# The opening of a one-core dynamic convolution with gated projection: softmax by lane, late zeros, x and weights in a new order, a buffer for the first group's rows

## The chip, the cores and the metric

One core of a Trainium2 chip runs the whole program. The time is the device time of one execution in microseconds (us), from fixed fp32 and 64-bit inputs in HBM to the fp32 result in HBM; three runs of the kernel before are given.

## The reference, cut to what matters

With B = 8 lanes of S = 4224 rows, D = 192 channels, H = 8 heads of 24 channels, K = 7 taps drawn per row and head, and 5 fixed taps per channel:

```
w   = softmax(weight_gen[b, s, h, :])                       # over 7 taps (the sum has 1e-9 added)
a   = sum_k w[b,s,h,k] * x[b, s-6+k, 24 channels of h]      # rows before 0 are zero
g   = sigmoid(sum_j conv_w[j] * a[b, s-4+j, :])             # 5 taps, per channel
out = (g * (a @ w_val)) @ w_out                             # 192 x 192 matrices
```

`conv_w`, `w_val` and `w_out` arrive as 64-bit floats and are turned into fp32 on the chip with integer operations.

## The kernel before, in words

**Work units.** The 4224 rows are cut into 36 groups: 80 rows, then 34 groups of 120, then 64. Two neighbouring groups make a pair (`Pair`); the first and the last group stand alone, so there are 19 pairs, 0 to 18. All 8 lanes go through a group together.

**Softmax parts.** Eleven `Softmax` parts `s0` to `s10` turn `weight_gen` into normalised taps. A part is loaded (`wt`), worked in place (max, subtract, exp on ScalarE, sum, reciprocal, multiply), gets its neighbours' edge rows (`halo`, L238, an SBUF to SBUF transfer), is spread into a padded layout (`spread`, L251, four copies), and stored to a DRAM buffer `z` (`store`, L265, four transfers). `s0` is worked in two halves of its rows (`h0`, `h1`), each with both of the two lanes that a partition holds. `s0` and `s1` are spread into parts of the tile `aA`, all later ones into `zt`. Rows of `z` end in a gap that must be zero; `clear_z` writes these from a zero tile.

**Banded weights and the first product.** `load_t` (L300, 7 or 9 transfers for a group) reads `z` with overlapping rows into one of two tiles `tb`, which gives a banded matrix; the parts of `tb` outside the band are cleared once (`tb_clear`). `load_x` brings the rows of `x` into one of three tiles `xt`. `bank` (L339) multiplies them, 128 small matmuls in four banks for a group, and `evac` (L354, ScalarE) copies the banks to `S`, `ringB`, `ringA`, `ringA`. The channels do not fit 128 partitions evenly: part of them goes by way of `S`, from which `move` (L362, L364, twelve transfers for a pair, GpSimd's queue) puts them into holes of the two rings. There is one `S`, and its next copy waits until the moves have read it.

**The second half of a pair, one and two steps later.** `tap0` (ScalarE, L380) and four `tap` (VectorE, L384) make the gate sum in `aA` and `aB`, `sigm` (L389) the sigmoid; `wva_`, `wvb_`, `wvm_`, `wvd_` (TensorE) the product with `w_val`; `gv` (VectorE, L435 to L443) multiplies the two and frees the banks `ps0` and `ps1`, which the next pair's `bank` writes; `omA` and `omB` (L451, L460) the product with `w_out`; `oev` and `store` take it out.

**Weights.** `order_weights` (six transfers, DRAM to DRAM), `load_weights` (six transfers, which wait for the first six), `convert_weights` (three blocks of eight VectorE operations), `place_weights` (ten ScalarE copies).

**Order.** Nothing is scheduled by a planner: every call `at(t, ...)` adds a step, the steps are sorted by their number t and issued in that order, and each engine works its own in order. SyncE, ScalarE and GpSimd each have a queue that issues transfers, and a transfer that waits holds up all that follows on its engine. Pairs have `when(q)` = 25, 30, 54, 79, then 24.5 more for each. The opening (L532 to L601) is written out by hand. In the opening before, GpSimd has the weights' twelve transfers ahead of `x`; SyncE has the loads of `s0`, `s1`, `s2` and both zeroings of `z` ahead of the first store.

Of the kernel before, what the change touches and what calls it, by code (L numbers as in the profile page):

```python
# [16 lines left out]
def tile_dynconv_gated_moe(  # L17
# [16 lines left out]
    P = 128  # L34
# [147 lines left out]
    class Softmax:  # L182
# [15 lines left out]
        def load(self, eng, lo=0, hi=None):  # L198
            R, n = self.R, (hi or self.m) - lo
            src = bass.AP(tensor=wg.tensor, offset=wg.offset + (self.r0 + lo) * ROW,  # L200
                          ap=[[R * ROW, NBL], [LQ * S * ROW, NL], [S * ROW, LQ], [1, n * ROW]])
            w = self.wt[:, 0:1]
            dst = bass.AP(tensor=w.tensor, offset=w.offset + lo * ROW,
                          ap=[[w.ap[0][0], P], [self.n * ROW, LQ], [1, n * ROW]])
            eng.dma_start(out=dst, in_=src)

        def own(self, lo=0, hi=None):
            hi = hi or self.m
            w = self.wt[:, :, lo:hi].rearrange("p l r (h k) -> p l (r h) k", k=K)
            m = self.mx[:, :, H * lo:H * hi]  # L210
            return w, m, m.unsqueeze(3).broadcast_to([P, LQ, (hi - lo) * H, K])

        def max(self, *rows):
            w, m, _ = self.own(*rows)
# [100 lines left out]
    class Pair:  # L315

        def __init__(self, q, ms):
            self.q, self.g = q, [gr[m] for m in ms]
            self.s = self.g[0].s
            self.n = sum(g.n for g in self.g)  # L320
            self.base = SLOT * (q % 2) + HALO
            self.lp = LH // len(self.g)
            self.w = self.lp * self.n
            self.pieces = LH // self.lp
            self.aA = aAs[(q + 2) % 3][:, 0:L * self.n]
            self.aB = aBs[q % 3][:, 0:LH * self.n]
# [17 lines left out]
        def evac(self, gi, kind, b):  # L344
# [188 lines left out]
    half = s0.m // 2  # L533
    h0, h1 = (0, half), (half, s0.m)
# [6 lines left out]
    at(0.3, clear_z, 0, 0, 320, SP)  # L541
    at(0.35, s2.load, SP)
# [74 lines left out]
    for q, pr in enumerate(pairs + [None, None]):  # L617
# [33 lines left out]
        if p1:  # L651
# [6 lines left out]
            st(6.5, p1.wvm_)  # L658
# [47 lines left out]
```

## Time and profile before

| | us |
|---|---|
| median of 3 runs (527.23, 529.28, 530.59) | 529.28 |
| the profiled execution, its own time | 531.67 |
| span of the profiled execution | 529.9 |
| VectorE busy | 425.9 (80%) |
| TensorE busy / weight loads | 457.3 (86%) / 334.9 (63%) |
| ScalarE busy / GpSimd busy | 314.8 (59%) / 312.9 (59%) |

All times in the text are us from the start of the span of this one execution. Over the whole span a mean share hides that the program has an opening, in which the first groups are prepared, and then a repeated pattern of pairs; the two are read apart by asking for windows of the span. An engine name with a q (SPq, ACTq, POOLq) is that engine's queue issuing a transfer; DVE is VectorE, ACT ScalarE, POOL GpSimd, SP SyncE, PE TensorE.

### The profile page before, as it was taken

The numbers are of one execution on the slowest core, as the hardware profiler recorded it, in microseconds if no ns is written. First come the engines' busy times: TensorE is split into PE (matmuls) and PEld (weight loads), VectorE is DVE, ScalarE is ACT, GpSimd is POOL, SyncE is SP. The second block draws the span as 40 slices with busy tenths as digits, with TensorE's granted clock in tenths as the row PEclk, the third lists the DMA queues.
The fourth block names the chain that finished last, engine by engine and source line by source line (L and its number), as shares of the span: only waits on it lengthen the run. The fifth ranks groups of instructions, "written<-read, shape, count | busy, mean of one in ns | idle before, by whom it ended". The sixth has DMA issues, their size and how long they took to land.

```text
span 529.9 us, 15947 instructions
## 1 busy us (share of the span) xinstructions
PE 457.3 (86%) x6546; PEld 334.9 (63%) x6546; DVE 425.9 (80%) x351; ACT 314.8 (59%) x434; POOL 312.9 (59%) x546
## 2 busy tenths in 40 slices
PE   7016569597979999999799999999899999999996
PEld 3016455556667767685668575868485858586584
DVE  5856749998978798889789897999699959695960
ACT  5513584766466747664766667675758474655532
POOL 8768597447563847384747566574738384816400
PEclk9557779799979999999999999999999999999999
DMA  8987878778888778968888888789786968664344
GB/s 252 220 220 195 195 222 210 210 159 228 274 238 198 206 250 232 224 188 268 226 231 223 244 239 220 230 242 251 214 263 173 264 177 245 163 185 103 93 113 114
DMA packets 90935, 111.33 MB, mean 210 GB/s; under 512 B 18473, under 2 KB 79248, under 8 KB 90862
## 3 DMA queue, kind: packets, MB, share of 16 engines
q1 hardware_dynamic: 67516, 73.14, 49.3%
q0 software_dynamic: 21904, 35.95, 26.6%
q10 hardware_dynamic: 1442, 1.21, 1.1%
q8 instruction: 52, 0.85, 0.7%
q14 instruction: 21, 0.17, 0.1%
HBM read 59.80 MB, written 41.17 MB: 191 GB/s over the span
## 4 chain that ended last, share of the span: by engine, by line
PE 31%; issue 21%; POOL 18%; DMA 13%; DVE 9%; ACT 7%; POOLq 0%; ACTq 0%; DVEq 0%
PE ps L339 11%; PE ps L451 8%; POOL xt L286 8%; PE ps L460 5%; DMA ringA<-S 5%; POOL ringA L362 5%; POOL ringB L364 4%; DMA xt<-in_x_dram 4%; DVE aA L435 3%; PE ps L416 3%; DVE aB L443 3%; ACT aA L389 2%; DVE aA L384 2%; PE ps L411 1%; DMA wt<-wt 1%
## 5 line engine op out<-in xcount | busy, mean ns | idle before, releaser
L339 PE MATMUL ps<-tb,xt 126*32 126x120 f32 (+2 forms) x4608 | 148.0, 287 | 52.1 <-DMA xt<-in_x_dram 26.5
L339 PEld LDWEIGHTS ps<-tb,xt 126*32 126x32 f32 x4608 | 136.3, 115 | 62.7 <-issue 41.9
L286 POOL DMA_DIRECT2D xt<-in_x_dram x272 | 158.9, 620 | 11.4 <-issue 3.2
L384 DVE SCALAR_TENSOR_TENSOR aA<-ringA,wf,aA 128x1920 f32<-128x1920 f32 (+2 forms) x76 | 157.3, 2070 | 5.7 <-DMA xt<-in_x_dram 3.6
L364 POOL DMA_DIRECT2D ringB<-S x76 | 42.1, 558 | 149.0 <-ACT ringB L354 99.3
L451 PE MATMUL ps<-wf,aA 128*120 128x192 f32 (+2 forms) x576 | 111.6, 342 | 14.1 <-DVE aA L435 7.0
L451 PEld LDWEIGHTS ps<-wf,aA 128*120 128x120 f32 (+2 forms) x576 | 93.5, 190 | 28.8 <-DVE aB L443 11.6
L466 ACT COPY ot<-ps 120x768 f32<-120x768 f32 (+2 forms) x72 | 55.9, 801 | 67.9 <-PE ps L460 57.1
L362 POOL DMA_DIRECT2D ringA<-S x152 | 81.8, 544 | 17.2 <-DMA ringB<-S 6.3
L384 DVE SCALAR_TENSOR_TENSOR aB<-ringB,wf,aB 128x960 f32<-128x960 f32 (+2 forms) x76 | 86.9, 1144 | 2.0
L435 DVE TENSOR_TENSOR aA<-ps,aA 128x960 f32<-128x960 f32 (+2 forms) x36 | 39.3, 1131 | 49.9 <-ACT aA L389 29.6
L416 PE MATMUL ps<-ringA,wva 128*128 128x480 f32 (+2 forms) x144 | 61.8, 571 | 0.0
L460 PE MATMUL ps<-wf,aB 64*120 64x192 f32 (+2 forms) x576 | 60.0, 336 | 0.9 <-ACT ot L466 0.9
L460 PEld LDWEIGHTS ps<-wf,aB 64*120 64x120 f32 (+2 forms) x576 | 46.8, 183 | 17.1 <-issue 15.4
L354 ACT COPY ringA<-ps 128x480 f32<-128x480 f32 (+2 forms) x72 | 36.2, 554 | 32.7 <-PE ps L339 32.7
L380 ACT ACTIVATE aA<-ringA,wf 128x960 f32<-128x960 f32 (+2 forms) x38 | 39.1, 1031 | 18.0 <-DMA ringA<-S 18.0
L354 ACT COPY S<-ps 128x480 f32<-128x480 f32 (+2 forms) x36 | 19.9, 553 | 48.1 <-PE ps L339 41.0
L416 PEld LDWEIGHTS ps<-ringA,wva 128*128 128x128 f32 x144 | 25.8, 189 | 35.7 <-issue 21.7
L261 ACT COPY zt<-wt 128x512 f32<-128x512 f32 (+4 forms) x36 | 30.3, 920 | 15.8 <-DMA tb<-z 8.5
L411 PE MATMUL ps<-ringA,wvm 128*32 128x480 f32 (+2 forms) x304 | 33.6, 537 | 0.0
L428 PE MATMUL ps<-ringB,wvb 64*128 64x480 f32 (+2 forms) x144 | 33.5, 581 | 0.0
L389 ACT ACTIVATE aA<-aA 128x1920 f32<-128x1920 f32 (+2 forms) x19 | 32.1, 1688 | 0.8 <-DVE aA L384 0.7
(61 smaller groups left out, 358.7 us busy)
## 6 DMA issues: line engine op xcount, KB each, us to landing
xt<-in_x_dram POOLq DMA_DIRECT2D x272, 94.5 KB, 3.7
out_dram<-ot SPq DMA_DIRECT2D x68, 360.0 KB
tb<-z SPq DMA_DIRECT2D x235, 74.4 KB
z<-zt SPq DMA_DIRECT2D x28, 306.0 KB
wt<-in_weight_gen_dram SPq DMA_DIRECT2D x7, 896.0 KB
ringA<-S POOLq DMA_DIRECT2D x136, 30.0 KB, 3.6
tb<-z SPq DMA_DIRECT2D x70, 52.1 KB
wt<-wt SPq DMA_DIRECT2D x8, 294.0 KB
```

Of the source, the lines that this page charges most:

```text
L286: eng.dma_start(out=self.xb[0:G * NW, j, 0:D], in_=src)
L339: nc.tensor.matmul(out=pa[Q * c:Q * c + Q, n * l:n * l + n], lhsT=g.xb[0:k, LH * u + l, C * h:C * h + Q], rhs=t[:, (LH * u + l) // LQ, PAD ...
L354: nc.scalar.copy(out=dst, in_=pa)
L362: nc.gpsimd.dma_start(out=ringA[q:q + h, LH * u:LH * u + LH, p0:p0 + n], in_=St[p:p + h, :, 0:n])
L364: nc.gpsimd.dma_start(out=ringB[HD * u + q:HD * u + q + h, :, p0:p0 + n], in_=St[p:p + h, :, 0:n])
L384: nc.vector.scalar_tensor_tensor(out=a, in0=self.src(g, j), scalar=cw[:, g, j:j + 1], in1=a, op0=ALU.mult, op1=ALU.add)
L389: nc.scalar.activation(out=a, in_=a, func=AF.Sigmoid)
L416: nc.tensor.matmul(out=self.v01(e)[:, u], lhsT=wva, rhs=self.A(e, u), start=True, stop=False)
L435: nc.vector.tensor_tensor(out=a, in0=self.v01(e), in1=a, op=ALU.mult)
L451: nc.tensor.matmul(out=ps[b][0:n, u, D * t:D * t + D], lhsT=g[:, u, t], rhs=woa, start=first and t == 0, stop=not first, skip_group_check= ...
L460: nc.tensor.matmul(out=ps[b][0:n, u, D * t:D * t + D], lhsT=g[hs, t], rhs=wob[hs], start=first and t == 0, stop=not first, skip_group_chec ...
L466: nc.scalar.copy(out=ots[0:n, 2 * e + k], in_=ps[b][0:n, :, 0:2 * D])
```

## The change

- `s0` is worked in two halves by lane (lane 0, lane 1) and no longer by rows; each half is then one unbroken stretch of `wt` and `mx`.
- The zeros of the first `z` (rows 0 to 320) go out on ScalarE's queue after the exp of the first half; those of the second `z` (rows 0 to 256) on SyncE's queue after the loads of `tb` for group 1, its second part (rows 256 to 512) from 47.0 to `when(2) + 13`.
- `s2` is loaded after `s0`'s store; its edge rows go by SyncE and no longer GpSimd; its max to multiply come before the conversions of the weights.
- GpSimd clears all four parts of `tb0` (ScalarE cleared two), brings `x` of groups 0 and 1, clears the ring edges and `zt`, and only then orders the weights; it loads them after `s1`'s edge rows and ahead of `x` of group 2.
- Three of `s0`'s four spread copies and all four of `s1`'s are VectorE's (two and two before).
- All 24 conversions stand together at 26 to 28, ahead of `s3`'s max and subtract; `s3`'s exp stands with `s2`'s spread and `place_weights` behind group 2's `evac` and ahead of pair 0's `tap0`; `s3`'s sum stands between pair 0's taps and its `gv`, reciprocal and multiply behind that `gv`.
- Pair 0 uses the free tile `aB2` in place of `S`.

```diff
-        def load(self, eng, lo=0, hi=None):
+        def load(self, eng, l0=0, l1=LQ):
...
-        def own(self, lo=0, hi=None):
+        def own(self, l0=0, l1=LQ):
+            w = self.wt[:, l0:l1, 0:self.m].rearrange("p l r (h k) -> p l (r h) k", k=K)
+            m = self.mx[:, l0:l1]
...
+            self.S = St if q else aBs[2][:, 0:LH * self.n].rearrange("p (l n) -> p l n", n=self.n)
...
-    h0, h1 = (0, half), (half, s0.m)
+    h0, h1 = (0, 1), (1, 2)
     at(0.0, s0.load, SP, *h0)
     at(0.1, s0.load, SP, *h1)
     at(0.2, s1.load, SP)
-    at(0.3, clear_z, 0, 0, 320, SP)
-    at(0.35, s2.load, SP)
     at(0.4, lambda: G_.memset(aAt[:, 0:(s0.R + s1.R) * DATA], 0.0))
-    at(1.0, order_weights)
-    tb_clear(0, 0, 2.0, G_)
-    tb_clear(0, 1, 2.1, G_)
+    for u in range(NL):
+        tb_clear(0, u, 2.0, G_)
-    at(3.0, load_weights)
     at(4.0, gr[0].load_x, G_)
     at(5.0, gr[1].load_x, G_)
-    at(5.5, clear_z, 1, 0, 256, SP)
+    at(5.1, lambda: G_.memset(ringA[:, :, 0:HALO], 0.0))
+    at(5.1, lambda: G_.memset(ringB[:, :, 0:HALO], 0.0))
+    at(5.2, lambda: G_.memset(zt, 0.0))
+    at(5.3, order_weights)
     steps(s0, "max sub exp", 4.1, *h0)
+    at(4.13, clear_z, 0, 0, 320, A)
-    spread(s0, 11.0, (A, V, A, V))
+    spread(s0, 11.0, (A, V, V, V))
     at(11.1, s0.store, (SP, A))
-    tb_clear(0, 2, 11.5, A)
-    tb_clear(0, 3, 12.1, A)
+    at(11.2, s2.load, SP)
     at(13.0, s1.halo, (G_,))
-    at(13.1, lambda: G_.memset(ringA[:, :, 0:HALO], 0.0))
-    at(13.1, lambda: G_.memset(ringB[:, :, 0:HALO], 0.0))
+    at(13.1, load_weights)
     at(13.2, gr[2].load_x, G_)
+    tail(s3, 13.3)
...
-            at((14.0, 28.0, 29.0)[k] + 0.01 * i, lambda f=f: f(V))
-            at(t + 0.01 * w, gr[gi].load_t, s0, w, lo, hi, (SP, A)[w % 2])
-    spread(s1, 24.9, (A, A, V, V))
+            at(t + 0.01 * w, gr[gi].load_t, s0, w, lo, hi, (SP, A)[(w + (gi == 1)) % 2])
+    at(24.2, clear_z, 1, 0, 256, SP)
+    steps(s2, "max sub", 24.6)
+    at(24.8, s2.exp)
+    spread(s1, 24.9, (V, V, V, V))
+    steps(s2, "sum recip norm", 25.0)
+            at(26.0 + k + 0.01 * i, lambda f=f: f(V))
     at(28.5, s1.store, (SP,))
-    tail(s3, 26.0)
-    at(37.0, lambda: G_.memset(zt, 0.0))
+    at(29.2, s2.halo, (SP,))
     at(29.5, s3.load, SP)
-    steps(s2, "max sub", 32.5)
+    steps(s3, "max sub", 33.0)
+    spread(s2, 36.51)
-        at(33.35 + 0.001 * i, f)
-    at(32.6, s2.exp)
-    steps(s2, "sum recip norm", 32.7)
-    at(33.0, s2.halo, (G_,))
-    steps(s3, "max sub", 44.0)
-    spread(s2, 45.0)
-    at(46.0, s2.store, (SP,))
+        at(36.56 + 0.001 * i, f)
+    at(36.6, s3.exp)
+    at(36.9, s2.store, (SP,))
+    at(38.2, s3.sum)
+    steps(s3, "recip norm", 41.0)
-    at(46.9, s3.exp)
-    at(47.0, clear_z, 1, 256, 512, SP)
+    at(when(2) + 13.0, clear_z, 1, 256, 512, SP)
-    steps(s3, "sum recip norm", when(1) + 20.6)
...
-            st(6.5, p1.wvm_)
+            st(6.5 if q > 1 else 6.9, p1.wvm_)
```

## Rows read from the trace of the kernel before

**Rows 1.** Windows: length, engines' busy us, PE clock, DMA share, GB/s.
```profile
0.00:40.00 40.00, 12.21 (x130) 7.85 (x134) 25.65 (x42) 16.32 (x17) 30.89 (x51) 0.67 0.89 231
127.60:465.60 338.00, 322.20 (x4686) 236.26 (x4684) 291.70 (x209) 217.88 (x294) 202.34 (x358) 0.99 0.82 227
```
**Rows 2.** TensorE timeline: start, length, operation [idle before]; groups 0, 2, 3, 5.
```profile
37.15 4.22 PE L339 MATMUL ps<-tb,xt 126*32 126x80 f32 x128 [26.48 <-DMA xt<-in_x_dram]
...
51.43 5.22 PE L339 MATMUL ps<-tb,xt 126*32 126x120 f32 x128 [2.41 <-DMA tb<-z]
...
65.38 5.04 PE L339 MATMUL ps<-tb,xt 126*32 126x120 f32 x128 [5.74 <-DMA ringA<-S]
...
98.64 5.41 PE L339 MATMUL ps<-tb,xt 126*32 126x120 f32 x128 [5.32 <-DMA tb<-z]
```
**Rows 3.** Timeline, VectorE: the first softmax part, by halves of its rows.
```profile
6.10 1.09 DVE L215 TENSOR_REDUCE mx<-wt 128x128 f32<-128x896 f32 x1 [3.17 <-DMA wt<-in_weight_gen_dram]
...
9.32 1.09 DVE L215 TENSOR_REDUCE mx<-wt 128x128 f32<-128x896 f32 x1 [1.01 <-ACT wt L223]
...
18.32 1.09 DVE L236 TENSOR_TENSOR wt<-wt,mx 128x896 f32<-128x896 f32 x1
```
**Rows 4.** ScalarE's exp line to 60: queue waits, ns, first to last.
```profile
L223 ACTq EVENT_SEMAPHORE  x3: 17/17/17, 4.8 to 22.6; - x3
```
**Rows 5.** Timeline, SyncE's queue: first stores of z, first loads of tb.
```profile
21.03 1.22 SPq L272 DMA_DIRECT2D z<-aA  x2
28.72 9.95 SPq L313 DMA_DIRECT2D tb<-z  x9
```
**Rows 6.** Transfers in 0 to 80: count, KB each, median us to landing.
```profile
xt<-in_x_dram POOLq DMA_DIRECT2D x40, 94.5 KB, 4.7
...
z<-zero SPq DMA_DIRECT2D x2, 816.0 KB
...
ot<-cd POOLq DMA_DIRECT2D x2, 2.5 KB, 6.3
...
cd<-in_moe_conv_w_dram POOLq DMA_DIRECT2D x1, 1.9 KB, 7.1
```
**Rows 7.** Timeline, GpSimd: two clears of tb, wt's edges, pair 1's late moves.
```profile
6.74 3.72 POOL L510 MEMSET tb<- 128x2142 f32 x2
10.52 1.25 POOL L527 MEMSET wt<- 32x672 f32 x2
...
63.38 3.27 POOL L362 DMA_DIRECT2D ringA<-S  x6 [3.12 <-DMA wt<-wt]
```
**Rows 8.** VectorE timeline: conversions (first, last of 16), taps, s3, taps.
```profile
37.55 0.35 DVE L137 TENSOR_SCALAR wf<-ot 128x384 uint32<-128x384 uint32 x1
...
44.25 0.56 DVE L148 SCALAR_TENSOR_TENSOR wf<-ot,wf 128x384 uint32<-128x384 uint32 x1
...
58.71 3.65 DVE L384 SCALAR_TENSOR_TENSOR aA<-ringA,wf,aA 128x640 f32<-128x640 f32 x4 [3.64 <-DMA xt<-in_x_dram]
...
66.28 2.02 DVE L215 TENSOR_REDUCE mx<-wt 128x256 f32<-128x1792 f32 x1
...
76.93 2.02 DVE L227 TENSOR_REDUCE mx<-wt 128x256 f32<-128x1792 f32 x1 [6.58 <-ACT wt L223]
...
83.04 8.97 DVE L384 SCALAR_TENSOR_TENSOR aA<-ringA,wf,aA 128x1920 f32<-128x1920 f32 x4
```
**Rows 9.** ScalarE timeline: group 1's S, tap0, s2's spread, s3's exp.
```profile
49.25 0.56 ACT L354 COPY S<-ps 128x480 f32<-128x480 f32 x1 [7.08 <-DMA ringA<-S]
...
57.59 1.02 ACT L380 ACTIVATE aA<-ringA,wf 128x320 f32<-128x320 f32 x2
...
71.83 2.06 ACT L261 COPY zt<-wt 128x256 f32<-128x256 f32 x4
...
75.20 1.70 ACT L223 ACTIVATE wt<-wt 128x1792 f32<-128x1792 f32 x1
```
**Rows 10.** place_weights in one window: length, ScalarE busy, PE clock, DMA share, GB/s.
```profile
51.00:54.00 3.00, 1.60 (x10) 0.51 0.92 315
```

More of the change, by code (lines that the diff above doesn't have):

```diff
@@ L196, in __init__ @@
             self.z = z[:, 0:R * self.row].rearrange("p (r c) -> p r c", r=R)
-        def load(self, eng, lo=0, hi=None):
[L199 to L204, printed above, removed]
-            eng.dma_start(out=dst, in_=src)
@@ L207, in own @@
-        def own(self, lo=0, hi=None):
[L208 to L214, printed above, removed]
+        def load(self, eng, l0=0, l1=LQ):
+            R, m = self.R, self.m
+            src = bass.AP(tensor=wg.tensor, offset=wg.offset + (l0 * S + self.r0) * ROW,
+                          ap=[[R * ROW, NBL], [LQ * S * ROW, NL], [S * ROW, l1 - l0], [1, m * ROW]])
+            w = self.wt[:, l0:l0 + 1]
+            dst = bass.AP(tensor=w.tensor, offset=w.offset,
+                          ap=[[w.ap[0][0], P], [self.n * ROW, l1 - l0], [1, m * ROW]])
+            eng.dma_start(out=dst, in_=src)
@@ L215, in max, with sub @@
+        def own(self, l0=0, l1=LQ):
+            w = self.wt[:, l0:l1, 0:self.m].rearrange("p l r (h k) -> p l (r h) k", k=K)
+            m = self.mx[:, l0:l1]
+            return w, m, m.unsqueeze(3).broadcast_to([P, l1 - l0, self.m * H, K])
+        def max(self, *ls):
+            w, m, _ = self.own(*ls)
             nc.vector.tensor_reduce(out=m, in_=w, axis=AX.X, op=ALU.max)
-        def sub(self, *rows):
-            w, _, m = self.own(*rows)
+        def sub(self, *ls):
+            w, _, m = self.own(*ls)
@@ L219, in sub, with exp, sum @@
             nc.vector.tensor_tensor(out=w, in0=w, in1=m, op=ALU.subtract)
-        def exp(self, lo=0, hi=None):
-            w = self.wt[:, :, lo:hi or self.m].rearrange("p l r c -> p l (r c)")
+        def exp(self, l0=0, l1=LQ):
+            w = self.wt[:, l0:l1, 0:self.m].rearrange("p l r c -> p l (r c)")
             nc.scalar.activation(out=w, in_=w, func=AF.Exp)
-        def sum(self, *rows):
-            w, m, _ = self.own(*rows)
+        def sum(self, *ls):
+            w, m, _ = self.own(*ls)
@@ L227, in sum, with recip, norm @@
             nc.vector.tensor_reduce(out=m, in_=w, axis=AX.X, op=ALU.add)
-        def recip(self, *rows):
-            m = self.own(*rows)[1]
+        def recip(self, *ls):
+            m = self.own(*ls)[1]
             nc.vector.tensor_scalar(out=m, in0=m, scalar1=1e-9, scalar2=None, op0=ALU.add)
             nc.vector.reciprocal(out=m, in_=m)
-        def norm(self, *rows):
-            w, _, m = self.own(*rows)
+        def norm(self, *ls):
+            w, _, m = self.own(*ls)
             nc.vector.tensor_tensor(out=w, in0=w, in1=m, op=ALU.mult)
@@ L352, in evac @@
             else:
-                dst = St[:, :, p0:p0 + n]
+                dst = self.S[:, :, p0:p0 + n]
             nc.scalar.copy(out=dst, in_=pa)
@@ L361, in move @@
             if g == 0:
-                nc.gpsimd.dma_start(out=ringA[q:q + h, LH * u:LH * u + LH, p0:p0 + n], in_=St[p:p + h, :, 0:n])
+                nc.gpsimd.dma_start(out=ringA[q:q + h, LH * u:LH * u + LH, p0:p0 + n], in_=self.S[p:p + h, :, 0:n])
             else:
-                nc.gpsimd.dma_start(out=ringB[HD * u + q:HD * u + q + h, :, p0:p0 + n], in_=St[p:p + h, :, 0:n])
+                nc.gpsimd.dma_start(out=ringB[HD * u + q:HD * u + q + h, :, p0:p0 + n], in_=self.S[p:p + h, :, 0:n])
         def halo(self, g):
@@ L515, in tile_dynconv_gated_moe, with steps @@
     V, A, G_, SP = nc.vector, nc.scalar, nc.gpsimd, nc.sync
-    def steps(p, names, t, *rows):
+    def steps(p, names, t, *ls):
         for i, f in enumerate(names.split()):
-            at(t + 0.01 * i, getattr(p, f), *rows)
+            at(t + 0.01 * i, getattr(p, f), *ls)
     def spread(p, t, engs=(A, A, A, A)):
@@ L530, in tb_clear @@
         at(t, lambda: clear(tb[i], u, c0, c1, eng))
-    half = s0.m // 2
-    h0, h1 = (0, half), (half, s0.m)
+    h0, h1 = (0, 1), (1, 2)
     at(0.0, lambda: V.memset(zero, 0.0))
```

4 lines of the change are left out of this document (2 added, 2 removed).

## The prediction

> **What bounds the kernel now.** I read the windows first, the engines' timelines second, and the landings of transfers last. In the first 40 us the DMA engines are 0.89 busy at 231 GB/s while VectorE works 25.65 us of 40 and TensorE 12.21 [rows 1]: the opening waits for data. In the repeated part, 338 us for 13 pairs from pair 4's start to pair 17's, VectorE is 86% busy and TensorE 95%, at 26.0 us a pair [rows 1]. No step there reads a clock, each waits for engines and buffers; so an opening that hands over d us earlier should end d us earlier, if all that pair 3 needs comes earlier too. The change touches only the opening (and two later zeros), so I price the hand-over.
>
> The starts of the first products tell the opening's course: group 0 at 37.15, group 2 at 51.43, group 3 at 65.38, group 5 (pair 3) at 98.64 [rows 2]. Group 3 could not start before VectorE had multiplied pair 0's banks free. Group 5 followed on pair 1's gate work on VectorE, which began at 83.04 [rows 8] though pair 0's was over at 66.28 [rows 8]. What lay between is the softmax of `s3`: max and subtract from 66.28, then idle 6.58 for an exp on ScalarE, then 76.93 to 83.04 for sum, reciprocal and multiply [rows 8]. That exp, at 75.20, stood behind `s2`'s spread at 71.83 and `tap0` of pair 1 [rows 9]. From 83.04 on VectorE goes from pair to pair with taps of 9 us each [rows 8]. **The date of pair 1's taps on VectorE, 83.04, is what I forecast.**
>
> **The change part by part.**
>
> *First softmax by lane.* The first max began at 6.10, when both halves had landed, though the first had by 4.8, where ScalarE's queue passed its wait for it [rows 3, 4]; the second max waited 1.01 for the exp of the other half [rows 3], and the first sum as long again for the second exp. Halves by rows interleave in a partition; halves by lane do not, so all three waits should go: 1.3 + 1.0 + 1.0 = 3.3 us. Three spread copies on VectorE beside one on ScalarE end about when two beside two did, or 0.3 earlier: 0.2. Stores start at 17.5 and not 21.03 [rows 5]. They took 7.7 us to let the loads of `tb` go (28.72) [rows 5]; with less queued ahead it could be 5, with the zeros now issued around 8 on the same engines it could be 9. I keep 7.7: group 0 at 37.15 - 3.5 = 33.6.
>
> *GpSimd's queue.* This pays for it. GpSimd is free at 3.1 (six transfers of about 0.6 before the clears at 6.74 [rows 7]). Then four clears of `tb0` 7.4, edges 1.25 [rows 7], small ones 0.3: 12.1. Fifteen `x` transfers at 0.6 (a move takes 3.27/6 [rows 7], these a little more): 21.1. Ring edges and `zt` (2448 against 2142 columns) 2.4: 23.5. Six weight transfers 3.7: 27.2; `s1`'s edge rows are ready by then. The loading of the weights waits for the last of the six, issued at 26.6 and landing 7.1 later [rows 6]: 33.7; its six take until 37.4 and the last lands 6.3 later [rows 6]: 43. Meanwhile `x` of group 2: a GpSimd transfer waits for the one eight before it (the move at 63.38 waited 3.12 for the edge rows issued eight earlier [rows 7]), so its last goes at 43 and lands 4.7 later [rows 6]: 47.7. The nearest rows bound each of the three landings between 4.7 [rows 6] and the stores' 7.7 [rows 5]; that is the largest unknown.
>
> *Conversions.* VectorE waits for 43, then does one small block of 1.6 (eight short operations) and two of 3.6 (37.55 to 44.81 for both [rows 8]): 51.9. `s3`'s max and subtract behind them 4.1 [rows 8]: 56.0. Before, the conversions were hidden behind the wait for `z`; here they hide behind group 2.
>
> *Pair 0's tap0.* It moves behind more of ScalarE's work. Group 2 starts between 47.7 (its `x`) and 51.4 as before (its `tb`, now behind a zeroing on SyncE): I take 49.5. Before, `tap0` followed 6.2 us after that start (57.59 [rows 9] less 51.43): 55.7. Now `s2`'s spread 2.06, `place_weights` 1.60, `s3`'s exp 1.70 come first [rows 9, 10]: `tap0` at 61.1, **3.4 later than before**. Exp needs 56.0 and does not wait. The taps and `gv` of pair 0 end 3.4 later, at 69.7, and `s3`'s sum of 2.0 in between makes 71.7; group 3 starts near 70.8 and not 65.38. This loses nothing, since the next copies to `S` before were held until past 76 by that same exp.
>
> *What VectorE no longer does.* After pair 0's `gv` only `s3`'s reciprocal and multiply are left: 83.04 - 76.93 - 2.05 = 4.1 [rows 8]. Pair 1's taps start at 75.8: 83.04 - 75.8 = **7.2 earlier**. Their rows must be there: pair 0's moves go at 44.3 behind `x` of group 2, twelve at 0.55, then eight `x` transfers, to 55.7; pair 1's twelve moves end at 62.3, landing some 4.7 later as the `x` transfers do [rows 6], and `tap0` of pair 1 (behind pair 0's sigmoid, 68.5 to 72) is in time. The 3.12 wait and the wait for `s2`'s multiply go with the edge rows' move to SyncE.
>
> *S for pair 0.* Group 1's copy to `S` waited 7.08 for pair 0's moves [rows 9]. With moves at 44 to 51 that wait would now reach 53; the spare tile removes it. It gains nothing by itself against 51.43, but without it group 2 would be late.
>
> *Zeros and `s2` later, clears to GpSimd:* their bytes leave the first 20 us and come back in 30 to 45, beside `tb`; I count zero, with -2 to +4 as bounds through group 2's start (47.7 to 53.5). The other load order on two queues: zero.
>
> Sum: 531.67 - 7.2 = 524.5 for the profiled execution; that one lies 2.4 above the median shown, so **522.1 as a median**.
>
> **The rivals.**
>
> *Slower: late weights hold VectorE.* Three GpSimd steps hang in a row (order, load, `x` of group 2), and VectorE, ScalarE and the moves stand behind them. The sum has 13.4 us for the first two landings. If they take 12 us each, as the DMA share of 0.89 [rows 1] and the extra `tb`, zeros and edge rows of that stretch allow, conversions end at 62.5, `s3`'s subtract at 66.6, exp and `tap0` at 68.4, pair 1's taps at 83.1 and their moves (last at 73, after `x` at 59) no earlier: gain nil; at 15 each, 89, the time is 535. It decides from 12 each. Against it: 7.1 and 6.3 were measured at the same DMA share. The Trainium skill's page "DMA: Bandwidth & Descriptors", section "Rules for kernel authors", says to issue a transfer early and wait on it late so that its fixed cost overlaps; by that rule moving the weights back from 3 to 23 us is wrong. The trace agrees only in part: of the weights issued at 3, two of three blocks were converted from 37.55 on [rows 8], so the early issue bought little there. Chance 0.15.
>
> *Gain given back at SyncE.* The second half of the second zeroing (816 KB [rows 6]) stood in an idle stretch; it now follows `s3`'s stores, and the loads of `tb` for group 7 must wait for it. 816 KB at 231 GB/s [rows 1] is 3.5 us. Where that load is what group 7 waits for, 3.5 of 7.2 are lost: 525.6. For: SyncE's queue is issuing most of the time there. Against: group 7 had VectorE's `gv` before it as well. Chance 0.25.
>
> *More.* If the lighter first 20 us let `z` land in 5 us and the weights in 5 each, group 2 starts at 47, `s3`'s subtract ends by 53, `tap0` comes at 58.6, pair 1's taps at 73.3; and if group 3 and the moves follow, sigmoid and `tap0` of pair 1 lie near 70: gain 10 to 11, 519. Chance 0.17.
>
> *It doesn't do what it says:* if operations on separate lanes still wait for each other, 2.0 of the 3.3 stays, but the store is not what decides pair 1's taps: 522 to 523. It is inside the forecast.
>
> **How the numbers follow.** Forecast 0.43, more 0.17, given back 0.25, slower 0.15. A measurement of this kernel tells about 1% (5.3 us) from no change. Faster by over 1%, below 524.0: the forecast but for its upper edge (0.38) and more (0.17): 0.55. Within: given back 0.25, that edge 0.05 = 0.30. Slower, over 534.6: the rival has its threshold case within 1%, but a longer one, or a stall that I did not see, beyond: 0.15. The range goes from 514 (more, with group 2 some 4 us sooner still) to 531 (given back and group 2 at 53.5, or weights at 12 us each).
>
> **What would show it.** Right: the first max near 4.8 and no wait before the second; stores of `z` near 17.5; a first conversion near 43 with VectorE idle before it; `tap0` of pair 0 at 58 to 63; pair 1's taps at 72 to 78; group 5 near 92; from there a constant lead. Wrong: conversions past 55; pair 1's taps waiting for moves; a lead that shrinks between group 5 and group 9, with SyncE's loads after the zeroing as the wait that ends last.

## The result, and the profile after

The changed kernel takes **535.64 us** (median; 530.84 to 543.85), the kernel before 529.18 in the same series (525.37 to 533.12): a ratio of **1.010, 95% interval 1.007 to 1.013**. It is about 1% slower; 522 had been forecast. Ratios here leave out disturbed executions, so they can differ from the ratio of the two medians.

Its profiled execution took 530.84, the shortest of its series and 4.8 under the median; that of the kernel before was 2.5 over its own. So the two spans (529.1 and 529.9) hide the difference, and I read dates and stretches, with a second profile of each kernel beside them. Columns of the timelines: start, duration, engine, line, operation, out<-in, shapes, count, and in brackets the idle time before and what ended it.

VectorE of the changed kernel in the opening:

```profile
4.70 1.09 DVE L214 TENSOR_REDUCE mx<-wt 128x128 f32<-128x896 f32 x1 [1.77 <-DMA wt<-in_weight_gen_dram]
6.83 1.08 DVE L214 TENSOR_REDUCE mx<-wt 128x128 f32<-128x896 f32 x1
...
40.77 0.17 DVE L137 TENSOR_SCALAR wf<-ot 128x10 uint32<-128x10 uint32 x1 [1.60 <-DMA ot<-wd]
...
59.78 2.02 DVE L214 TENSOR_REDUCE mx<-wt 128x256 f32<-128x1792 f32 x1 [9.96 <-DMA wt<-in_weight_gen_dram]
...
66.53 3.65 DVE L385 SCALAR_TENSOR_TENSOR aA<-ringA,wf,aA 128x640 f32<-128x640 f32 x4 [2.67 <-DMA ringA<-S]
...
80.07 8.97 DVE L385 SCALAR_TENSOR_TENSOR aA<-ringA,wf,aA 128x1920 f32<-128x1920 f32 x4
```

The first stage came as forecast [rows 3]: first max at 4.70, no wait before the second. The conversions began at 40.77, earlier than the 43 forecast. But behind them VectorE stood 9.96 us for the **load of `s3`**. Pair 1's taps began at 80.07: 3.0 before the first profile of the kernel before [rows 8], and 0.8 before its second one:

```profile
80.85 4.47 DVE L384 SCALAR_TENSOR_TENSOR aA<-ringA,wf,aA 128x1920 f32<-128x1920 f32 x2
95.84 1.44 PE L339 MATMUL ps<-tb,xt 126*32 126x120 f32 x28 [4.95 <-DMA tb<-z]
```

SyncE's queue of the changed kernel in the same stretch:

```profile
17.44 1.22 SPq L271 DMA_DIRECT2D z<-aA  x2
...
26.40 7.64 SPq L312 DMA_DIRECT2D tb<-z  x8
34.08 0.74 SPq L180 DMA_DIRECT2D z<-zero  x1
39.31 6.34 SPq L271 DMA_DIRECT2D z<-aA  x4
45.76 4.19 SPq L312 DMA_DIRECT2D tb<-z  x5
...
51.70 0.69 SPq L205 DMA_DIRECT2D wt<-in_weight_gen_dram  x1
```

The four stores of `s1` take 6.34 us to issue (3.19 in the kernel before). The list of waits of this queue (what waited, for what: us in total, times, longest) says why, for 30 to 80 us:

```profile
SPq L271 <- DMA tb<-z: 4.6, 2, 4.4
SPq L271 <- DMA z<-zero: 3.9, 1, 3.9
```

One store, the last, waited 3.9 us for the moved zeroing; the 4.4 us stand before the first. `s3`'s load went at 51.70 and ended VectorE's wait at 59.78. ScalarE and TensorE follow:

```profile
63.89 1.70 ACT L222 ACTIVATE wt<-wt 128x1792 f32<-128x1792 f32 x1 [2.36 <-DVE wt L218]
65.50 1.00 ACT L381 ACTIVATE aA<-ringA,wf 128x320 f32<-128x320 f32 x2
```

```profile
33.07 1.25 PE L340 MATMUL ps<-tb,xt 126*32 126x80 f32 x29 [22.13 <-DMA tb<-z]
51.64 1.74 PE L340 MATMUL ps<-tb,xt 126*32 126x120 f32 x28 [5.31 <-DMA tb<-z]
75.12 1.23 PE L340 MATMUL ps<-tb,xt 126*32 126x120 f32 x20 [9.75 <-DVE aA L436]
96.55 1.23 PE L340 MATMUL ps<-tb,xt 126*32 126x120 f32 x34
128.06 1.13 PE L340 MATMUL ps<-tb,xt 126*32 126x120 f32 x32
```

These are groups 0, 2, 3, 5 and 7. Group 0 is 4.1 earlier than in [rows 2], group 2 no earlier, group 3 almost 10 us later. Group 7 of the kernel before:

```profile
127.58 3.88 PE L339 MATMUL ps<-tb,xt 126*32 126x120 f32 x128
```

The lead is gone there; the second profile of the kernel before has 124.17.

What bounds this stretch shows in the windows (length, busy time of the engines, granted clock of TensorE, share and GB/s of the DMA engines). Kernel before, then changed kernel:

```profile
0.00:20.00 20.00, 9.36 (x42) 4.97 (x42) 13.24 (x16) 9.08 (x9) 16.62 (x25) 0.84 0.90 252
20.00:40.00 20.00, 2.85 (x88) 2.88 (x92) 12.41 (x27) 7.24 (x9) 14.27 (x26) 0.50 0.88 210
40.00:60.00 20.00, 14.90 (x339) 12.90 (x330) 11.25 (x19) 8.72 (x25) 15.55 (x28) 0.81 0.82 211
60.00:80.00 20.00, 9.47 (x188) 8.39 (x192) 13.07 (x16) 13.34 (x19) 16.16 (x26) 0.70 0.76 199
```

```profile
0.00:20.00 20.00, 9.63 (x42) 5.06 (x42) 16.54 (x20) 9.90 (x10) 19.34 (x27) 0.85 0.66 176
20.00:40.00 20.00, 4.49 (x128) 4.23 (x128) 13.17 (x18) 2.79 (x6) 15.93 (x26) 0.55 0.99 236
40.00:60.00 20.00, 10.68 (x256) 10.18 (x256) 8.65 (x25) 6.04 (x13) 14.55 (x26) 0.83 0.91 245
60.00:80.00 20.00, 9.91 (x148) 6.92 (x152) 16.94 (x18) 11.29 (x25) 15.83 (x28) 0.66 0.86 225
```

The change took 76 GB/s x 20 us = 1.5 MB out of the first 20 us and put them into the next 60, where the DMA engines are 0.86 to 0.99 busy.

The rest of the program, as differences between first products of groups, in us (from TensorE's timeline of each profiled execution; those of the experiments stand here too):

| kernel | start of group 5 | 5 to 9 | 9 to 31 | 31 to 33 | 33 to the end |
|---|---|---|---|---|---|
| before, first profile | 98.6 | 59.5 | 282.5 | 25.0 | 64.3 |
| before, second | 95.8 | 57.3 | 282.3 | 24.3 | 64.3 |
| changed, first profile | 96.6 | 58.8 | 281.2 | 27.9 | 64.6 |
| changed, second | 99.0 | 60.2 | 283.9 | 28.6 | 64.5 |
| first half of zeroing early | 93.4 | 61.3 | 284.7 | 26.8 | 64.5 |
| both halves early | 92.1 | 60.6 | 281.4 | 27.4 | 64.5 |
| both early, edge rows ahead | 93.0 | 56.1 | 279.5 | 28.1 | 64.5 |
| changed, `s2`'s edge rows on GpSimd | 97.8 | 60.2 | 284.7 | 24.3 | 64.7 |
| before, split by lane alone | 95.4 | 57.3 | 281.1 | 24.8 | 64.3 |

The stretch from 9 to 31 scatters by some 5 us whatever the kernel. Three others differ by kernel: the opening, groups 5 to 9, and groups 31 to 33. In the first two the two profiles of one kernel already differ by 1 to 3 us, so a difference of that size says nothing there. The experiments take them in this order.

### The profile page after: what moved, and what is told of

The parts are those of the page before. It is cut to its first block, busy times and chain, and to the rows that moved or that the text cites. A ratio compares the mean times of both kernels' runs of the same rounds, so it can differ in the third digit from the quotient of the medians.

```text
span 529.1 us, 15941 instructions
## 1 busy us (share of the span) xinstructions
PE 458.8 (87%) x6546; PEld 332.7 (63%) x6546; DVE 427.8 (81%) x354; ACT 307.3 (58%) x427; POOL 318.4 (60%) x546
## 4 chain that ended last, share of the span: by engine, by line
PE 30%; issue 20%; DMA 16%; POOL 12%; DVE 12%; ACT 6%; SPq 2%; ACTq 1%; POOLq 0%; DVEq 0%
PE ps L340 12%; PE ps L452 7%; POOL xt L285 6%; PE ps L461 5%; POOL ringA L363 4%; DMA ringA<-S 3%; PE ps L417 3%; DMA tb<-z 3%; DVE aB L444 2%; DVE aA L436 2%; POOL ringB L365 2%; DMA out_dram<-ot 2%; DVE aA L385 2%; DMA ringB<-S 2%; DMA xt<-in_x_dram 2%
## 5 line engine op out<-in xcount | busy, mean ns | idle before, releaser
L340 PE MATMUL ps<-tb,xt 126*32 126x120 f32 (+2 forms) x4608 | 146.1, 284 | 45.6 <-DMA tb<-z 32.4
L340 PEld LDWEIGHTS ps<-tb,xt 126*32 126x32 f32 x4608 | 134.0, 114 | 57.3 <-issue 44.2
L285 POOL DMA_DIRECT2D xt<-in_x_dram x272 | 161.4, 600 | 10.5 <-PE ps L429 3.1
L365 POOL DMA_DIRECT2D ringB<-S x72 | 40.2, 562 | 148.4 <-ACT ringB L355 117.7
L452 PEld LDWEIGHTS ps<-wf,aA 128*120 128x120 f32 (+2 forms) x576 | 92.2, 188 | 29.2 <-DVE aB L444 13.9
L467 ACT COPY ot<-ps 120x768 f32<-120x768 f32 (+2 forms) x72 | 56.0, 801 | 71.8 <-PE ps L461 60.6
L363 POOL DMA_DIRECT2D ringA<-S x144 | 77.7, 547 | 14.7 <-DMA ringB<-S 10.7
L461 PE MATMUL ps<-wf,aB 64*120 64x192 f32 (+2 forms) x576 | 61.2, 341 | 0.9 <-ACT ot L467 0.9
L461 PEld LDWEIGHTS ps<-wf,aB 64*120 64x120 f32 (+2 forms) x576 | 47.7, 187 | 17.2 <-issue 15.6
L355 ACT COPY S<-ps 128x480 f32<-128x480 f32 (+1 forms) x35 | 19.5, 558 | 55.3 <-PE ps L340 55.3
```

What stands on the lines that cost most here:

```text
L285: eng.dma_start(out=self.xb[0:G * NW, j, 0:D], in_=src)
L340: nc.tensor.matmul(out=pa[Q * c:Q * c + Q, n * l:n * l + n], lhsT=g.xb[0:k, LH * u + l, C * h:C * h + Q], rhs=t[:, (LH * u + l) // LQ, PAD ...
L452: nc.tensor.matmul(out=ps[b][0:n, u, D * t:D * t + D], lhsT=g[:, u, t], rhs=woa, start=first and t == 0, stop=not first, skip_group_check= ...
L461: nc.tensor.matmul(out=ps[b][0:n, u, D * t:D * t + D], lhsT=g[hs, t], rhs=wob[hs], start=first and t == 0, stop=not first, skip_group_chec ...
L467: nc.scalar.copy(out=ots[0:n, 2 * e + k], in_=ps[b][0:n, :, 0:2 * D])
```

## The experiments

Lines starting with - and + are against the kernel named.

**The changed kernel again.** No edit.

> The changed kernel once more, for a second profile. Theory A (the opening: s3's load stands on SyncE's queue behind the first half of the second zeroing and the first loads of tb for group 2, VectorE waits for it some 10 us, and pair 1's taps come only 3 us earlier than before): VectorE again idle 8 to 12 us before s3's max, near 60, pair 1's taps at 79 to 82. Theory B (the lead is lost later, in the part that repeats): the opening as in the first profile within 1 us, and the difference to it, if this execution is longer, grows from pair to pair. Time 534 to 538 in both.

537.51 us, ratio 1.015 (1.011 to 1.019). Pair 1's taps 2.0 later than in its first profile, group 5 at 98.95: together with the second profile of the kernel before (below), no gain at group 5 is left of the 6.6 forecast.

**`s3`'s load ahead of the zeroing.** Changed kernel:

```diff
-    tail(s3, 13.3)
-    at(29.5, s3.load, SP)
+    at(24.195, s3.load, SP)
+    tail(s3, 29.05)
```

> Changed kernel with s3's load issued on SyncE just ahead of the first half of the second zeroing instead of behind the loads of tb for group 2, and s3's tail clear behind that on its own engine. Theory A: s3's max follows the conversions at about 50 to 52 with little idle time in place of 59.8, s3's exp near 56, pair 0's tap0 near 58 to 60 (65.5 now), pair 1's taps at 73 to 76 (80.1 now), and the time falls by 4 to 7 us to 529 to 531. Theory B: the opening dates move as said but the lead is gone by group 7, and the time stays at 533 to 537.

538.53 us, ratio 1.018 (1.012 to 1.025): no gain. The load was early, and the wait moved. TensorE and VectorE of this run:

```profile
58.70 2.18 PE L340 MATMUL ps<-tb,xt 126*32 126x120 f32 x37 [11.29 <-DMA tb<-z]
```

```profile
52.78 2.02 DVE L214 TENSOR_REDUCE mx<-wt 128x256 f32<-128x1792 f32 x1 [3.03 <-POOL wt L528]
71.48 3.65 DVE L385 SCALAR_TENSOR_TENSOR aA<-ringA,wf,aA 128x640 f32<-128x640 f32 x4 [14.62 <-DMA ringA<-S]
```

`s3`'s max came at 52.8, but group 2's loads 5 us later, so group 2 at 58.7 and pair 0's taps at 71.5. Another order on SyncE's queue makes no room: one of the two is late.

**First half of the zeroing early.** Changed kernel:

```diff
-    at(24.2, clear_z, 1, 0, 256, SP)
+    at(5.5, clear_z, 1, 0, 256, SP)
```

> Changed kernel with the first half of the second zeroing back at its old place, early on SyncE. Theory A: z lands 2 to 4 us later (group 0 near 35 to 37), but s3's load and the loads for group 2 go 8 to 11 us earlier: s3's load lands near 50, group 2 starts at 46 to 49, pair 0's tap0 near 58 to 60, pair 1's taps near 74 to 76, time 528 to 532. Theory B: no more than 2 us gained, 533 to 537.

530.25 us, ratio 1.002 (0.997 to 1.007): by the medians 5 to 7 us faster than the changed kernel, the intervals only just apart (up to 1.0067 here, from 1.0072 there). Two rows of VectorE, and the issue of `s3`'s load:

```profile
55.77 2.02 DVE L214 TENSOR_REDUCE mx<-wt 128x256 f32<-128x1792 f32 x1 [5.27 <-DMA wt<-in_weight_gen_dram]
...
76.06 6.72 DVE L385 SCALAR_TENSOR_TENSOR aA<-ringA,wf,aA 128x1920 f32<-128x1920 f32 x3
```

```profile
49.62 0.69 SPq L205 DMA_DIRECT2D wt<-in_weight_gen_dram  x1
```

Pair 1's taps at 76.06, close to the 75.8 forecast. So **this one edit cost the opening its gain**. Group 5 came at 93.4, 3.2 and 5.6 us ahead of the changed kernel's two profiles. `s3`'s max came 4.0 us earlier than in the first of them: 2.1 because its load was issued earlier (49.62 and not 51.70), 1.9 because the load ended VectorE's wait 6.2 us after its issue and not 8.1. By these dates the turn on SyncE's queue and the slower landing carry about half each.

**The same zeroing on GpSimd's queue.** Changed kernel, to tell the bytes from the wait on SyncE:

```diff
-    at(24.2, clear_z, 1, 0, 256, SP)
+    at(5.31, clear_z, 1, 0, 256, G_)
```

> Changed kernel with the first half of the second zeroing on GpSimd's queue right behind the ordering of the weights, near 27, so that the same bytes fall in the same stretch but none of the transfers of SyncE and ScalarE waits for it in its turn of eight. Theory A1 (the bytes cost, the DMA engines have no room between 20 and 60): s3's max still near 58 to 60, pair 1's taps at 79 to 82, time 533 to 537. Theory A2 (the waiting turn on SyncE costs, 3.9 us on s1's fourth store and what stands behind it): s3's max near 55, pair 1's taps near 76, 530 to 532.

540.29 us, ratio 1.013 (1.005 to 1.022). It went at 27.77, among the first loads of `tb`, and TensorE's first row was

```profile
40.59 1.69 PE L340 MATMUL ps<-tb,xt 126*32 126x80 f32 x44 [30.37 <-DMA tb<-z]
```

7.5 later than in the changed kernel; `s3`'s max came at 65.05. No transfer of SyncE waits for it in turn, and it is worse: A2's dates fail, and the bytes beside full DMA engines cost by themselves (7.5 for the 3.5 that they need at 231 GB/s). But they went 6.3 us earlier than in the changed kernel, into group 0's loads, so this run does not say that the turn on SyncE costs nothing. The Trainium skill, "DMA: Bandwidth & Descriptors", section "Issuing engines are not separate DMA queues", says that transfers of ScalarE, SyncE and GpSimd interleave on the same DMA engines, so that another issuer saves only the time to issue; these rows agree.

**More of it early.** The zeros of the first `z` and `s2`'s load as well (at 0.3 and 0.35 on SyncE):

> Changed kernel with the first half of the second zeroing, the zeros of the first z and the load of s2 all back in the first microseconds, on SyncE. Theory A1 (room of the DMA engines: the first 20 us of the changed kernel moved 176 GB/s against 252 before, and what was moved out of them comes back between 20 and 80): 248 GB/s or more in the first 20 us, s3's max at 50 to 54, group 5 at 90 to 92, time 524 to 529. Theory A2 (only the zeroing's turn matters): as with the first half alone early, group 5 near 93 and 529 to 531. If first loads of s0 or s1 are slowed, s0's stores come past 18.

529.04 us, ratio 1.001 (0.997 to 1.006). The first 20 us moved 238 GB/s, group 5 came at 93.94: no more than with the first half alone. These are A2's dates: the place of that zeroing costs, by its turn and by its bytes, and bringing the other displaced bytes back gained nothing more.

**The edit alone in the kernel before.**

```diff
-    at(5.5, clear_z, 1, 0, 256, SP)
+    at(24.2, clear_z, 1, 0, 256, SP)
```

> Kernel before with one edit of the change alone: the first half of the second zeroing behind the loads of tb for group 1. Theory A (in that place it holds SyncE and meets a stretch in which the DMA engines have no room): slower by 3 to 6 us, 533 to 536, group 5 at 101 to 104. Theory B (it hurts only together with the other edits, since kernel before has 6.6 us of idle VectorE between pair 0 and pair 1): within 1.5 us of kernel before.

533.17 us, ratio 1.004 (0.9995 to 1.008): not told from nothing. Group 5 came at 102.3, 3.6 or 6.4 later than in the two profiles; the date is as theory A had it, the time does not confirm it.

**Second half of the zeroing early**, and **both halves early**. Changed kernel:

```diff
-    at(when(2) + 13.0, clear_z, 1, 256, 512, SP)
+    at(47.0, clear_z, 1, 256, 512, SP)
```

> Changed kernel with the second half of the second zeroing back at its old place, ahead of s3's store, and not ahead of group 7's loads. Theory A: the opening is as in the changed kernel and the time falls by at most 2 us, to 533 to 536. Theory B (this half takes the lead away at group 7): group 7 starts 2 to 4 us earlier than now (128.1), and the time falls by 3 to 6 us, to 529 to 533.

534.50 us, ratio 1.012 (1.007 to 1.016). From group 5 to group 7 it took 28.3 us (group 7 at 124.53), against 31.5 and 31.6 in the two profiles of the changed kernel: about the 3.5 of the prediction's rival "Gain given back at SyncE". But from group 7 to group 9 it took 33.5, against 27.3 and 28.6, so that group 9 came at 157.98, between those two profiles (155.34 and 159.11). With the first half early as well:

> Changed kernel with both halves of the second zeroing at their old places (first half early on SyncE, second ahead of s3's store). Theory A (the loss is the first half, in the opening, and the second half costs group 7 another 3.5 us as the second halves' run showed): group 5 near 93 as in the run with the early first half, group 7 at 121 to 123 (125.8 there, 127.6 before), time 526 to 529. Theory B (a lead that reaches the part that repeats is lost there whatever it comes from): the same dates up to group 7, but time 529 to 532, with pairs 3 to 5 longer by as much.

529.44 us, ratio 1.000 (0.995 to 1.004). Group 7 at 120.33, 7.2 and 3.8 ahead of the two profiles of the kernel before; group 9 at 152.70, 5.4 and 0.4 ahead. The timeline of this run says where it went, by engine:

```profile
123.53 4.12 SPq L475 DMA_DIRECT2D out_dram<-ot  x3
127.76 1.70 SPq L244 DMA_DIRECT2D wt<-wt  x2
...
138.84 3.72 ACT L260 COPY zt<-wt 128x512 f32<-128x512 f32 x4 [7.19 <-DMA wt<-wt]
...
144.29 2.22 DVE L436 TENSOR_TENSOR aA<-ps,aA 128x960 f32<-128x960 f32 x2 [7.00 <-ACT aA L390]
...
146.57 1.95 PE L452 MATMUL ps<-wf,aA 128*120 128x192 f32 x5 [6.05 <-DVE aA L436]
```

A part's edge rows stand on SyncE behind three outputs and land 11 us after their issue. The spread waits 7.19 for them, the sigmoid stands behind it, and VectorE's `gv` and TensorE wait 7.00 and 6.05 in turn. Group 7 came even before theory A's 121 to 123. The time lies on the border of A and B; the trace sides with B.

**Edge rows ahead of the outputs**, from the fifth part on; with both halves early, and in the kernel before alone:

```diff
-        at(when(q - 2) + 3.3, p.halo, (SP,))
+        at(when(q - 2) + 3.3 if p is s3 else when(q - 3) + 20.95, p.halo, (SP,))
```

> Changed kernel with both halves of the second zeroing at their old places and, from the fifth softmax part on, the edge rows sent on SyncE right behind the multiply and no longer behind the previous pair's outputs. Theory A (the lead is lost at the spread, which waited 7.2 us for these rows in the run with both halves early, and with it the sigmoid, VectorE's gv 7.0 and TensorE 6.0): the wait of the spread near 144 falls under 4 us, group 9 at 148 to 151 (152.7), time 525 to 528. Theory B (SyncE's outputs come 2 us later for it, and other waits take the place): 528 to 532.

524.36 us in four executions, **ratio 0.987 (0.980 to 0.995)**: faster than both kernels.

```profile
136.32 3.79 ACT L260 COPY zt<-wt 128x512 f32<-128x512 f32 x4 [2.27 <-DMA wt<-wt]
```

The spread's wait is 2.27 and groups 5 to 9 take 56.1.

> Kernel before with the same move of the edge rows alone. Theory A: its spread waited 4.3 us for a load of tb and the rows there came from 134.8, so a part of this goes too: 0 to 3 us faster, 526 to 529. Theory B: 529 to 532, since the rows were not the last that was waited for.

527.71 us, ratio 0.997 (0.993 to 1.001); 5 to 9 took 55.3. A few us in the trace, not told from nothing in time.

**The kernel before again.**

> Kernel before once more, for a second profile. Theory A (a lead of 5 to 6 us at group 5 in the runs with the early zeroing is real): group 5 at 97 to 100, group 9 at 156 to 159, as in the first profile of kernel before. Theory B (the date of group 5 scatters by as much as the leads that were read): group 5 at 92 to 95 or past 102.

525.91 us in one run. Group 5 at 95.84, group 9 at 153.13, 3 and 5 us earlier than in the first profile: neither theory's date, between them.

**`s3`'s softmax order alone in the kernel before.**

```diff
-    steps(s3, "max sub", 44.0)
-    spread(s2, 45.0)
-    at(46.0, s2.store, (SP,))
-    at(46.9, s3.exp)
-    steps(s3, "sum recip norm", when(1) + 20.6)
+    steps(s3, "max sub", 33.1)
+    spread(s2, 36.51)
+    at(36.6, s3.exp)
+    at(36.9, s2.store, (SP,))
+    at(38.2, s3.sum)
+    steps(s3, "recip norm", 41.0)
-    at(37.0, lambda: G_.memset(zt, 0.0))
+    at(32.9, lambda: G_.memset(zt, 0.0))
```

> Kernel before with one edit of the change alone: s3's max and subtract behind s2's multiply, s2's spread and s3's exp ahead of pair 0's tap0, s3's sum between pair 0's taps and its gv, reciprocal and multiply behind that gv (and zt cleared earlier for it). Theory A (this edit gives the lead, as predicted: 4 us less between pair 0 and pair 1 on VectorE): group 5 at 93 to 96, time 524 to 529, 529 where the lead is lost at the spread near 144. Theory B (the lead comes from the first stage): group 5 at 97 to 100 or later, since pair 0's tap0 then waits for s3's load and exp; time 528 to 533.

530.50 us, ratio 0.999 (0.994 to 1.003); group 5 at 97.5, between the dates of the two profiles. Pair 1's taps came at 80.34 (83.04 and 80.85 in those two). The edit from which most of the 7.2 us were worked out gives nothing by itself that these runs resolve.

**Split by lane and spread on VectorE alone in the kernel before** (the softmax by lane, spread (A, V, V, V)).

> Kernel before with one edit of the change alone: first softmax by lane, and three of the first spread's four copies on VectorE. Theory A (the prediction's step: 3.5 us in the stores of z, but another date sets pair 1's taps): stores at 17 to 18 (21.0), group 0 at 33 to 35, group 5 at 95 to 99 as in kernel before, time 528 to 531. Theory B (the first stage gives the lead of 4 us that the runs with the early zeroing show at group 5): group 5 at 92 to 94, time 526 to 530.

526.57 us, **ratio 0.993 (0.989 to 0.998)**. SyncE's and TensorE's rows:

```profile
17.51 1.21 SPq L271 DMA_DIRECT2D z<-aA  x2
27.48 10.13 SPq L312 DMA_DIRECT2D tb<-z  x9
```

```profile
35.93 1.38 PE L338 MATMUL ps<-tb,xt 126*32 126x80 f32 x33 [25.72 <-DMA tb<-z]
```

The stores are 3.5 earlier as forecast, `z` takes 10.0 us from there to the first load and not 7.7 [rows 5], and the time falls by 0.7%. Theory A's dates held, but for group 0 (33 to 35); its time was too high. The stretches of this trace are within 1.2 us of those of the second profile of the kernel before, so where the 0.7% comes from is not shown.

**`s2`'s edge rows: GpSimd or SyncE.** Between groups 31 and 33 the changed kernels so far take 2 to 4 us longer, all but the one with the zeroing on GpSimd. ScalarE's and GpSimd's rows there, of the changed kernel, then of the kernel before:

```profile
445.39 0.56 ACT L355 COPY ringB<-ps 128x480 f32<-128x480 f32 x1
...
449.13 2.29 POOL L365 DMA_DIRECT2D ringB<-S  x4 [11.16 <-issue]
```

```profile
108.91 0.57 ACT L354 COPY ringB<-ps 128x480 f32<-128x480 f32 x1
...
112.40 0.58 POOL L364 DMA_DIRECT2D ringB<-S  x1 [13.36 <-issue]
...
449.30 0.57 ACT L354 COPY ringB<-ps 128x480 f32<-128x480 f32 x1
...
450.17 2.27 POOL L364 DMA_DIRECT2D ringB<-S  x4 [5.27 <-ACT ringB L354]
```

Before, the moves of pair 16 go 0.3 us after the copy that they need ends; after, 3.2 (449.13 against 445.39 + 0.56), for nothing that the profile names. In the kernel before such a wait, of 2.9, stands before pair 3's first move (112.40 against 108.91 + 0.57). The changed kernel with both transfers back on GpSimd:

```diff
-    at(29.2, s2.halo, (SP,))
+    at(29.2, s2.halo, (G_,))
```

> Changed kernel with s2's edge rows back on GpSimd (both transfers) and nothing else. Theory A: no 3.2 us wait before pair 16's moves, one of some 3 us elsewhere, near pair 3, as in kernel before; group 31 to 33 in 24 to 25 us; time 531 to 535, since the wait near pair 3 costs as well in part. Theory B: 535 to 538 and 28 us from group 31 to 33; the moves of x and of pair 0 come later by the wait for s2's multiply.

531.71 us, ratio 1.006 (1.001 to 1.010). The reverse, in the kernel before:

```diff
-    at(33.0, s2.halo, (G_,))
+    at(33.0, s2.halo, (SP,))
```

> Kernel before with s2's edge rows on SyncE and nothing else. Theory A: the 2.9 us wait before pair 3's moves goes and one of 3.2 us before pair 16's comes; group 31 to 33 takes 28 us and not 24.5; time 529 to 533. Theory B: no wait there, 527 to 530.

533.29 us, ratio 1.003 (0.999 to 1.008). The moves of pair 16, with the edge rows on GpSimd in the changed kernel and on SyncE in the kernel before:

```profile
452.24 1.74 POOL L365 DMA_DIRECT2D ringB<-S  x3 [5.55 <-ACT ringB L355]
```

```profile
456.38 1.75 POOL L364 DMA_DIRECT2D ringB<-S  x3 [11.15 <-issue]
```

Both directions: 0.3 us and 24.3 from group 31 to 33 in the one (with 2.9 before pair 3's first move), 3.2 and 26.3 in the other (with 0.3 there, and 2.6 before the fourth of these moves). This edit alone brings the wait to pair 16. The ratios shift as theory A says, by 0.4 to 0.9% and by 0.3%, at the edge of what is resolved.

**One of the two transfers on GpSimd**, in the version with both halves early and edge rows ahead (`(SP, G_)`):

> The run with both halves of the zeroing early and the edge rows ahead of the outputs (524.4), with one of the two transfers of s2's edge rows back on GpSimd, so that its queue holds one transfer more. Theory A (the place of the 3.2 us wait depends on how many transfers GpSimd has issued): pair 16's moves go 0.3 us after their copy, group 31 to group 33 takes 24 to 25 us and not 28, time 521 to 523. Theory B (the wait belongs to that place for another reason): 3.2 us again, 523 to 526.

526.23 us, ratio 0.992 (0.988 to 0.996). 3.2 us again: one transfer more does not take the wait away from pair 16. The kernel with the zeroing on GpSimd, which had one more too, had the wait at neither place.

The traces hold a count all the same. In every profile of this document GpSimd stands four times for 2.1 to 3.2 us, longer where it had to wait anyway, each time when its queue (q0 on the profile's page) has moved about 5,000 packets more, which is some 120 transfers. In the changed kernel these are at 112.31 (5,041 packets), 226.12 (10,032), 335.45 (15,072) and 449.13 (20,016); in the kernel before at 112.40, 226.98, 335.71 and 443.15 (5,152, 10,048, 15,040 and 19,957). The first of the changed kernel, and the fourth of the kernel before:

```profile
112.31 0.56 POOL L365 DMA_DIRECT2D ringB<-S  x1 [2.58 <-issue]
```

```profile
443.15 1.75 POOL L286 DMA_DIRECT2D xt<-in_x_dram  x3 [2.64 <-PE ps L339]
```

So `s2`'s edge rows carry no wait from one place to another: with their two transfers on GpSimd the fourth wait falls on a transfer of `x`, 7 us ahead of pair 16's moves, and without them on the first of these moves. The kernel with the zeroing on GpSimd had its fourth at 450.10, on `x` too.

**Two versions to keep.** The version with both halves early and edge rows ahead, with `s2`'s edge rows on GpSimd:

> Changed kernel with both halves of the zeroing at their old places, the edge rows from the fifth part on ahead of the outputs, and s2's edge rows on GpSimd as before. Theory A (the wait near pair 16 goes, the one near pair 3 comes, and that one is hidden in part as in kernel before): 522 to 525, a ratio of 0.985 to 0.991, group 31 to 33 in 24 to 25 us. Theory B (what is saved there is paid at pair 3 and by x of group 2, which comes later): 525 to 528.

525.59 us, ratio 0.993 (0.989 to 0.996); group 31 to 33 in 24.4. The dates are theory A's, the time is B's: beside 524.36 and 526.23 the shorter stretch gains nothing that is resolved. And the kernel before with only the split by lane, the spread on VectorE and the edge rows ahead:

> Kernel before with the first softmax by lane, three of its spread copies on VectorE, and the edge rows from the fifth part on ahead of the previous pair's outputs; nothing else of the change. Theory A (the two parts add: 3.0 and 1.8 us alone): 524 to 526, a ratio of 0.989 to 0.994, so that the rest of the change gives nothing on top. Theory B (the later weights, order of sums and buffer of the change give the rest): 526 to 528, and 2 to 3 us slower than the other kernel of this call.

526.67 us, ratio 0.985 (0.976 to 0.994). That ratio rests on two of the six executions (517.77 and 524.91); the medians of all give 0.995. The intervals of the two overlap: as far as these runs resolve it, two small edits give what the best versions give, and the rest of the change adds nothing.

## Why the prediction was wrong

**Right:** the first max (4.70; 4.8 forecast), the three waits, the stores (17.44; 17.5), GpSimd's queue up to the ordering of the weights (last `x` issued by 20.9; order from 23.1), and the weights, whose landings were if anything too dear (conversions at 40.77; 43). The rival with late weights did not come: VectorE waited 1.60 for them. The time lies where its 0.15 stood, for other reasons.

**The step that failed: "Zeros and `s2` later ... I count zero".** I bounded it by group 2's start (47.7 to 53.5), and that held (51.64). What I had not priced is what stands behind the zeroing on SyncE: `s1`'s stores, group 2's loads, `s3`'s load. My conversions step let `s3`'s max follow at 51.9; it came at 59.78. Pair 0's `tap0` at 65.50 (61.1) and pair 1's taps at 80.07 (75.8) were 4.4 and 4.3 late: some 2.1 by group 2's start, for which the sum took 49.5, and 2.36 by ScalarE's wait for `s3`'s subtract, where I had written "Exp needs 56.0 and does not wait". With that zeroing early the taps came at 76.06, though `s3`'s max, at 55.77, was still 3.9 behind the forecast. I had read the DMA share of 0.89 [rows 1] as the bound of the opening and then moved bytes inside it at no price.

**A reference of one profile.** The 7.2 us were taken off 83.04 [rows 8]; a second profile of the kernel before has 80.85, where VectorE's wait before `s3`'s sum is 3.81 and not 6.58. Up to a third of the forecast gain can be scatter of that row, and the sum then took off 2.4 more for the length of the same execution.

**"From there a constant lead" failed too.** The case "given back at SyncE" named a real place: groups 5 to 7 took 3.2 us less with the second half early, close to its price. But it was one of three. With group 7 earlier still, the edge rows take most of the lead back, and the move of `s2`'s edge rows, priced as a gain on GpSimd ("The 3.12 wait ... go"), brings a wait of that size to pair 16, where TensorE stood 2 us and then ran at a granted 0.83, a mean over its two levels of 1.2 and 2.4 GHz (changed kernel; columns as above; the kernel before has 1.00 in both):

```profile
450.00:460.00 10.00, 8.03 (x46) 4.78 (x44) 4.34 (x7) 5.07 (x8) 9.72 (x18) 1.00 0.61 154
460.00:470.00 10.00, 10.00 (x162) 8.73 (x164) 9.89 (x5) 4.70 (x8) 0.77 (x2) 0.83 0.73 213
```

**The sum as measured,** by the means of the two profiles of each kernel: opening +0.5 (97.7 against 97.2), groups 5 to 9 +1.1, 9 to 31 +0.2, 31 to 33 +3.6, rest +0.2: 5.6 against 6.5 in the medians. Two profiles a side leave 2 us open in the first three terms. The largest term is pair 16, where the fourth wait of GpSimd falls; the zeroing took the opening's gain. Of the opening, 4.6 us are the zeroing's (group 5 comes at 93.1 in the mean of the three runs with it early and the edge rows not moved); without it the lead would have been 4.1, not 7.2.

**Not settled:** what GpSimd does in these 3 us. Their place goes by the packets of its queue, about 5,000 from one to the next; why it does is not shown.

## What to carry to other kernels

Where the DMA engines are nine tenths busy, moving a transfer that nobody waits for is an edit with a price: look for what is issued or lands behind it in the new place, on all queues, and price that. The Trainium skill, "DMA: Bandwidth & Descriptors", section "Rules for kernel authors", advises to issue a transfer early and wait late, so that its fixed cost overlaps. Early was better here for the zeroing (5 to 7 us), though by the room on the DMA engines and the turn on SyncE; for the other zeros and `s2`'s load it made no difference that was measured. A lead in the opening is only worth what the next fixed wait of the repeated part leaves of it; look for that wait first, and take reference dates from more than one profile.

## What the runs showed of the hardware

- The same 816 KB of zeros cost group 0 nothing measurable at 3 us (it came at 33.1 to 34.0 with them there, at 33.1 and 33.5 without) and 7.5 us at 27.8 us, though at 231 GB/s they need 3.5.
- Transfers of SyncE ended the wait for them 8.1 us after their issue (`s3`'s load of 896 KB, 51.70 to 59.78) and 11 (edge rows, 127.8 to 138.8), against 4.7 to 7.7 in the rows of smaller transfers from which I had priced landings [rows 5, 6].
- GpSimd stands 2.1 to 3.2 us each time its queue has moved about 5,000 packets more (some 120 transfers), four times in every profile; two transfers more or fewer decide what falls on such a place, and whether it costs.
